# Second product of expert 0: seven products of token pairs for three of four batches, with the sums on GpSimd

## The chip, the cores and the metric

The kernel runs on 1 core of one Trainium2 chip. The metric is device time in microseconds (us); less is better. The engines are called as in the profile: PE (TensorE matmuls), PEld (TensorE weight loads), DVE (VectorE), ACT (ScalarE), POOL (GpSimd) and SP (SyncE).

## The reference

Block-sorted attention for 4 batches of 768 tokens, 8 heads of 64, is followed by a mixture of 8 experts in which every token goes through every expert, weighted by a balanced gate.

```python
def _attn_ref(q, k, v, sort_net):
    P = sort_net
    for _ in range(5):                       # softmax over rows, then columns summed to one
        ...
    k_sorted = np.einsum('bhij,bhjcd->bhicd', P, k_b).reshape(B, H, S, D)
    v_sorted = np.einsum('bhij,bhjcd->bhicd', P, v_b).reshape(B, H, S, D)
    ...                                      # softmax attention inside each block of 96 tokens

def _moe_ref(x, w_gate, w1, w2):             # x is [3072, 512]
    P = np.exp(x @ w_gate - max)
    for _ in range(8):                       # rows to one, columns to one, times N / E
        ...
    for e in range(E):
        h = np.maximum(x @ w1[e], 0.0)       # [3072, 1024]
        out += P[:, e:e + 1] * (h @ w2[e])   # [3072, 512]
```

## The kernel before

Matmuls take bf16 operands; results are gathered in float32 in SBUF, 24 tiles `osbl[:, t, :]` of 128 tokens and 512 columns, six to a batch.

**Stages.** Attention of the four batches comes first. Each batch is a list of steps in `attention`: `queries` (q0 to q3), `keys`, `scores`, `mix`, `turn` and `logits`, one of each for a pair of heads. In batches 2 and 3 (counted from 0) `queries` first has GpSimd copy a pair of heads into a small tile `qr` (two buffers), which TensorE then transposes. `sort_values` makes the sorted values of the next batch and sends them through eight DMAs (`vsb`, four issued by GpSimd, four by SyncE). `load_batch` and `load_w1`/`load_w2` are DMAs issued by GpSimd.

Expert 0 is woven into attention: `first_two` yields its steps for batches 0 and 1, in halves of 384 tokens, and `weave` takes a given number of them (`ns`) between attention steps. `hidden0` makes one block of 128 hidden features for 384 tokens (4 matmuls of 384 columns, then relu on ScalarE); `output0` makes one tile of results with 8 matmuls of 512 columns, in two steps of four. `keep` copies a result tile from PSUM to `osbl`. Batches 2 and 3 of expert 0 come after attention, in `last_two`, beside the gate's balancing (`balance`, a chain of small VectorE operations and matmuls), and batch 3's output is interleaved step by step with part of the first hidden stage of expert 1.

Experts 1 to 7 already multiply 2x2 blocks with seven products in place of eight (Strassen-Winograd) in both their products. The block sums that this needs are made on GpSimd for w1 (`sum_w`), w2 (`sum_w2`) and h (`sum_h`, tiles `hs`), and on VectorE for x (`sum_x`). `output7` makes two result tiles, `a` and `b`, out of seven products of 4 matmuls of 256 columns each.

**What sets the order.** Each engine runs its own instructions in the order of its queue. `pin` keeps an instruction in the order in which the program writes it; GpSimd's DMAs, copies for `build_r`, w1 and w2 sums are pinned, and so are most matmuls. `tc.issue_after` holds the first weight loads behind one copy. Before the w2 sums of expert 1 a pinned copy `held <- glog` (line 644) makes GpSimd wait for the balance, and `sums(8)` stands behind it at step 40 of the loop over `last_two`.

**The steady loop.** After that, for each of 21 passes (an expert and a third of the tokens), the outputs of one pass run beside the hidden steps of the next. In expert 1's passes `scale0` multiplies expert 0's result tiles by the gate, on ScalarE, for the tiles not yet multiplied when they were kept.

Of the kernel before, what the change touches and what calls it, by code (L numbers as in the profile page):

```python
# [1 line left out]

_os.environ.setdefault("NEURON_RT_ULTRASERVER_MODE", "4")
# [10 lines left out]
F32 = mybir.dt.float32  # L14
BF16 = mybir.dt.bfloat16
AF = mybir.ActivationFunctionType
AX = mybir.AxisListType
ALU = mybir.AluOpType
# [7 lines left out]
def kernel(  # L26
# [11 lines left out]
    nc = tc.nc  # L38
# [9 lines left out]
    wp = ctx.enter_context(tc.tile_pool(name="wp", bufs=2))  # L48
    wcp = ctx.enter_context(tc.tile_pool(name="wcp", bufs=1))
    xtp = ctx.enter_context(tc.tile_pool(name="xtp", bufs=1))  # L50
    actx = ExitStack()
    mps = actx.enter_context(tc.tile_pool(name="mps", bufs=2))
    kvp = actx.enter_context(tc.tile_pool(name="kvp", bufs=2))
# [30 lines left out]
    def load_w2(e):  # L84
        w2t[e] = (wq if e else wcp).tile([128, 8, Dm], BF16, name="w2e")
        pin(nc.gpsimd.dma_start(out=w2t[e],
                                in_=moe_w2[e].rearrange("(fb k) f -> k fb f", k=128)))
# [32 lines left out]
        nc.vector.reciprocal(out=cs, in_=cs)  # L120
        nc.vector.tensor_mul(Pt, Pt, mkap(cs, [cs.ap[0], cs.ap[1], [0, 8]]))

    Prep = perp.tile([32, 8, 8, 16], BF16)
    for eng, i0 in ((nc.vector.tensor_copy, 0), (nc.scalar.copy, 4)):
        eng(Prep[:, i0:i0 + 4], mkap(P, [P.ap[0], [8, 4], [1, 8], [0, 16]], off=i0 * 8))

    xtT = xtp.tile([128, 4, N], BF16)
    osbl = xtp.tile([128, NT, Dm], F32)
    glog = xtp.tile([128, NT, E], F32)
    xc = {0: xtp.tile([128, 3, 2, 512], BF16, name="xc0")}  # L130

# [166 lines left out]
            yield  # L298


    def hidden0(c0, hTs, hbank):
        for fb in range(8):
            hps = hbank()
            for kk in range(4):
                pin(nc.tensor.matmul(hps[:, 0:384], w1t[0][:, kk, fb * 128:(fb + 1) * 128],
                                     xtT[:, kk, c0:c0 + 384], start=(kk == 0), stop=(kk == 3)))
            nc.scalar.activation(out=hTs[:, fb, 0:384], in_=hps[:, 0:384], func=AF.Relu)  # L307
            yield

    def output0(c0, hTs, obank, done):  # L310
        for tt in range(3):
            oacc = obank()
            for fb in range(8):
                pin(nc.tensor.matmul(oacc, hTs[:, fb, tt * 128:(tt + 1) * 128],
                                     w2t[0][:, fb, :], start=(fb == 0), stop=(fb == 7)))
                if fb == 3:
                    yield
            done(c0 // 128 + tt, oacc)
            yield

    def keep(t, oacc):
        (nc.vector.tensor_copy if t < 12 else nc.scalar.copy)(osbl[:, t, :], oacc)

    def keep_scaled(t, oacc):
        nc.scalar.activation(out=osbl[:, t, :], in_=oacc, func=AF.Copy,
                             scale=glog[:, t, 0:1])

    wct = {}

# [36 lines left out]
    def weave(a, b, na, nb):  # L366

        t = 0
        for i in range(na):
            next(a, 0)  # L370
            while t * na < (i + 1) * nb:
                next(b, 0)
                t += 1

    with ExitStack() as c2:
        pa = c2.enter_context(tc.tile_pool(name="pa", bufs=8, space=bass.MemoryType.PSUM,
                                           reuse_waits="tile"))
        bank1 = lambda shape, dt: pa.tile(shape, dt, name="bank", tag="bank")
        ebank = lambda: bank1([128, 512], F32)
        def first_two():  # L380
            for c0 in range(0, 2 * S, 384):
                hTs = mps.tile([128, 8, 384], BF16, name="hTs")
                yield from hidden0(c0, hTs, ebank)
                yield from output0(c0, hTs, ebank, keep)

        ex = first_two()
        for _ in range(12):
            next(ex)
        for bb, ns in ((1, (5, 3, 3, 5)), (2, (5, 3, 2, 4)), (3, (5, 4, 0, 5))):
            at1 = attention(bb, bank1)  # L390
            weave(at1, ex, 5, ns[0])
            if bb + 1 < B:
                load_batch(bb + 1, [(x, 0, 8) for x in "vkq"])
                build_r(bb + 1, nc.gpsimd, 4)
            else:
                load_w1(1)
                sums = sum_w(1)
            weave(at1, ex, 3, ns[1])
            if bb + 1 < B:
                weave(sort_values(bb + 1, bank1), ex, 5, ns[2])  # L400
            else:
                for _ in sums:
                    pass
                x0 = sum_x(0)
                for _ in range(3):
                    next(x0)
            weave(at1, ex, 4, ns[3])
        for _ in ex:
            pass
# [2 lines left out]

    late = lambda name, bufs: ctx.enter_context(
        tc.tile_pool(name=name, bufs=bufs, reuse_waits="tile"))
    mpc, xcp, wq, wcq = late("mpc", 1), late("xcp", 2), late("wq", 2), late("wcq", 1)
    htp, fsp, hsp, w2q = late("htp", 2), late("fsp", 1), late("hsp", 3), late("w2q", 1)
    h3p = late("h3p", 2)
    bk = ctx.enter_context(tc.tile_pool(name="bk", bufs=5, space=bass.MemoryType.PSUM,
                                        reuse_waits="tile"))
    op = ctx.enter_context(tc.tile_pool(name="op", bufs=3, space=bass.MemoryType.PSUM,  # L420
                                        reuse_waits="tile"))
    load_w2(1)

    def bank():
        return bk.tile([128, 512], F32, name="bk")

    w2s = {}

    def sum_w2(e):
        w2s[e] = (w2q.tile([128, 4, 4, Dm // 2], BF16, name="w2s") if e % 2 else  # L430
# [104 lines left out]
        yield  # L535

    def gather(e, t, c, ps):
        o = osbl[:, t, c:c + ps.shape[-1]]
        nc.vector.scalar_tensor_tensor(out=o, in0=ps, scalar=glog[:, t, e:e + 1], in1=o,  # L539
                                       op0=ALU.mult, op1=ALU.add)  # L540

    def store(e, t):
        if e == E - 1:
            nc.sync.dma_start(out=out[t * 128:(t + 1) * 128, :], in_=osbl[:, t, :])

    hs = {}

    def sum_h(i, hT, f0=0, f1=4):

        if f0 == 0:  # L550
            hs[i] = hsp.tile([128, 3, 4, 128], BF16, name="hs")
        s1, s2, s4 = (hs[i][:, j, f0:f1] for j in range(3))
        a11, a21, a12, a22 = (hT[:, f + f0:f + f1, t + 128 * i:t + 128 * i + 128]
                              for f in (4, 0) for t in (0, 512))
        for a, b, o, c in ((a21, a22, ALU.add, s1), (s1, a11, ALU.subtract, s2),
                           (a12, s2, ALU.subtract, s4)):
            nc.gpsimd.tensor_tensor(out=c, in0=a, in1=b, op=o)  # L557
# [40 lines left out]

    def scale0(ts):
        for t in ts:  # L600
            nc.scalar.activation(out=osbl[:, t, :], in_=osbl[:, t, :], func=AF.Copy,
                                 scale=glog[:, t, 0:1])

    def units(e, p, hT, hold=lambda ins: ins):
        for i in range(4):
            yield from hidden(e, p, i, hT, hold)
# [7 lines left out]
            else:  # L614
                queue.pop(0)

    def last_two():
        for bb, done in ((2, keep), (3, keep_scaled)):
            hT = htp.tile([128, 8, 1024], BF16, name="hT")
            halves = [(bb * S + c, hT[:, :, c:c + 384]) for c in (0, 384)]  # L620
            for c0, hTs in halves:
                yield from hidden0(c0, hTs, bank)
            for c0, hTs in halves:
                yield from output0(c0, hTs, lambda: op.tile([128, Dm], F32, name="oacc"), done)

    tail0, chain = last_two(), balance()
    x1, x2 = sum_x(1), sum_x(2)
    works = {0: x0, 10: x1, 14: x1, 19: x1, 23: x1, 41: x2, 43: x2, 46: x2, 48: x2}
    first = None
    for n in range(56):  # L630
        next(tail0)
        if n == 28:
            hT = htp.tile([128, 8, 1024], BF16, name="hT")
            first = units(1, 0, hT, pin)
        if first:
            next(first)
            if n == 28 + 21:
                sum_h(0, hT, 0, 3)
        if n in works:
            next(works[n], 0)  # L640
        if n in (0, 2, 4, 6, 8, 11, 13, 15, 17, 20, 22, 24, 26, 29, 31, 33, 35, 37, 39):
            next(chain)
        if n == 40:
            pin(nc.gpsimd.tensor_copy(held, glog[0:96, NT - 1, 0:2]))
            sums(8)

    hTs = {0: hT}

# [8 lines left out]
    for n in range(1, 3 * (E - 1) + 1):  # L657
        e, p, hT = 1 + (n - 1) // 3, (n - 1) % 3, hTs[n - 1]
        d = 2 + n // 3
        fetch = n == 1 or n % 3 == 0 and d < E  # L660
        if fetch:
            load_w1(d)
            queue.append(sum_w(d))
        for i in range(4):
            if e == 1:
                scale0([t for t in (8 * p + i, 8 * p + 4 + i) if t < 18])
            if i == 0:
                sum_h(0, hT, 3)
            if i < 3:
                sum_h(i + 1, hT)  # L670
            elif n < 3 * (E - 1):
                sum_h(0, hTs[n], 0, 3)
            sums(1 + i // 2)
            for _ in output7(e, p, i, hT):
                next(ahead, 0)
        if fetch:
            load_w2(d)
            queue.append(sum_w2(d))
# [30 lines left out]
```

## Time and profile before

| what | value |
|---|---|
| median of 3 runs | 681.02 us (680.26 to 682.88) |
| the profiled execution | 680.63 us, of which 678.7 us from first to last instruction |
| PE busy | 654.8 us (96%) |
| DVE, ACT, POOL busy | 544.7, 298.5, 472.4 us |
| mean granted TensorE clock | 0.991 |
| attention of batch 1, 2, 3 starts | 45, 70, 93 us |
| attention ends, late part of expert 0 begins | 114 us |
| steady loop begins | 171 us |
| one pass of the steady loop | 24.3 us |

The times of the stages are read from the order of the matmuls in the timeline: transposes of queries open a batch's attention, and the last hidden matmul of the 28 that run beside batch 3's output closes the late part. All times inside the profile count from the start of the span.

### The profile page before, as it was taken

What the parts mean: (1) busy time and instruction counts of PE and PEld (TensorE: products, weight loads), DVE (VectorE), ACT (ScalarE), POOL (GpSimd) and SP (SyncE); (2) the same over time, 40 slices, a digit from 0 to 9 for tenths busy, and PEclk for the clock granted to TensorE, in tenths of its full rate; (3) what the DMA queues carried; (4) which work ended last, traced back from release to release, by engine and by line L of the source; (5) the groups of instructions that cost most, each with busy time, mean ns of one, the idle gap of its engine ahead of it and who ended that gap; (6) DMA issues with size and microseconds to landing.
All of it is one profiled execution on the core that took longest, in us unless ns stands there. A gap on an engine that the chain in (4) does not pass through costs nothing.

```text
span 678.7 us, 13239 instructions
## 1 busy us (share of the span) xinstructions
PE 654.8 (96%) x5108; PEld 436.7 (64%) x5108; DVE 544.7 (80%) x1154; ACT 298.5 (44%) x550; POOL 472.4 (70%) x499
## 2 busy tenths in 40 slices
PE   2989999999999999999999999999999999999996
PEld 1756766554666666666666666666666666666665
DVE  6727768663788889888888888888898888988885
ACT  3757764469533343434334343333433334333330
POOL 4542335007987988898997898689887989645744
PEclk9799999999999999999999999999999999999999
DMA  9898972101240340030303040034003220001223
GB/s 145 165 218 130 153 125 44 26 1 19 44 63 1 63 63 2 1 63 11 54 1 58 6 63 1 3 61 63 1 2 63 28 36 0 1 1 64 94 94 125
DMA packets 31759, 36.57 MB, mean 54 GB/s; under 512 B 2000, under 2 KB 24016, under 8 KB 31696
## 3 DMA queue, kind: packets, MB, share of 16 engines
q0 software_dynamic: 26400, 27.82, 25.8%
q1 hardware_dynamic: 5296, 7.90, 3.4%
q8 instruction: 40, 0.66, 0.4%
q14 instruction: 23, 0.19, 0.1%
HBM read 52.45 MB, written 6.29 MB: 87 GB/s over the span
## 4 chain that ended last, share of the span: by engine, by line
PE 72%; DVE 1%; POOL 1%; issue 0%; ACT 0%
PE oacc L572 37%; PE bk L487 35%; DVE osbl L539 1%; POOL hs L557 1%; DVE hT L523 0%; DVE hT L526 0%; ACT p L507 0%
## 5 line engine op out<-in xcount | busy, mean ns | idle before, releaser
L539 DVE SCALAR_TENSOR_TENSOR osbl<-oacc,glog,osbl 128x256 f32<-128x256 f32 (+1 forms) x504 | 262.4, 523 | 62.5 <-PE oacc L572 62.2
L487 PE MATMUL bk<-xtT,w1e 128*128 128x512 bf16 x504 | 149.7, 379 | 0.0
L557 POOL TENSOR_TENSOR hs<-hT 128x512 bf16<-128x512 bf16 (+2 forms) x105 | 99.6, 961 | 67.9 <-DVE hT L526 67.8
L572 PEld LDWEIGHTS <-hT 128*128 128x128 bf16 x1008 | 98.6, 98 | 64.8 <-issue 1.3
L572 PEld LDWEIGHTS <-hs 128*128 128x128 bf16 x1008 | 98.4, 98 | 64.2 <-POOL hs L557 1.5
L572 PE MATMUL oacc<-w2e,hT 128*128 128x256 bf16 x816 | 123.1, 273 | 0.8 <-ACT hT L529 0.5
L529 ACT ACTIVATE hT<-bk 128x512 bf16<-128x512 f32 x84 | 50.3, 599 | 158.2 <-PE bk L487 158.2
L557 POOL TENSOR_TENSOR hs<-hT,hs 128x512 bf16<-128x512 bf16 (+2 forms) x105 | 100.0, 959 | 4.9
L557 POOL TENSOR_TENSOR hs<-hs,hT 128x512 bf16<-128x512 bf16 (+2 forms) x105 | 100.0, 960 | 4.3 <-ACT hT L529 0.4
L487 PE MATMUL bk<-xc,wc 128*128 128x512 bf16 x336 | 99.9, 379 | 0.2 <-ACT p L507 0.2
L572 PE MATMUL oacc<-w2e,hs 128*128 128x256 bf16 x624 | 93.8, 273 | 0.9 <-POOL hs L557 0.9
L515 ACT COPY u<-bk 128x512 f32<-128x512 f32 x84 | 49.3, 587 | 95.4 <-PE bk L487 93.2
L487 PEld LDWEIGHTS <-w1e 128*128 128x128 bf16 x672 | 65.8, 98 | 10.4
L523 DVE CUSTOM_DVE_ANT_0 hT<-bk,p 128x512 bf16<-128x512 f32 x84 | 58.1, 692 | 11.5 <-ACT p L520 6.4
L533 DVE SCALAR_TENSOR_TENSOR h<-bk,hT 128x512 bf16<-128x512 f32 x84 | 57.2, 681 | 5.7 <-ACT hT L529 5.7
L520 ACT COPY p<-bk 128x512 f32<-128x512 f32 x84 | 49.4, 588 | 23.2 <-PE bk L487 23.2
L507 ACT COPY p<-bk 128x512 f32<-128x512 f32 x84 | 49.4, 588 | 20.3 <-PE bk L487 20.3
L511 DVE CUSTOM_DVE_ANT_0 hT<-bk,p 128x512 bf16<-128x512 f32 x84 | 57.2, 681 | 0.9 <-ACT hT L307 0.5
L526 DVE CUSTOM_DVE_ANT_0 hT<-bk,u 128x512 bf16<-128x512 f32 x84 | 57.1, 680 | 1.0 <-PE bk L487 1.0
L572 PE MATMUL oacc<-w2s,hs 128*128 128x256 bf16 x384 | 57.5, 273 | 0.1
L487 PEld LDWEIGHTS <-wc 128*128 128x128 bf16 x504 | 49.3, 98 | 8.0 <-issue 0.4
L487 PE MATMUL bk<-xc,w1e 128*128 128x512 bf16 x168 | 50.0, 379 | 0.0
(110 smaller groups left out, 820.6 us busy)
## 6 DMA issues: line engine op xcount, KB each, us to landing
w1e<-in_moe_w_dram POOLq DMA_DIRECT2D x8, 1024.0 KB, 8.2
w2e<-in_moe_w_dram POOLq DMA_DIRECT2D x8, 1024.0 KB, 9.0
out_dram<-osbl SPq DMA_DIRECT2D x24, 256.0 KB, 2.0
kvq<-in_v_dram POOLq DMA_DIRECT2D x3, 768.0 KB, 10.3
vsb<-vs SPq DMA_DIRECT2D x16, 97.5 KB, 4.7
vsb<-vs POOLq DMA_DIRECT2D x16, 97.5 KB, 4.3
kvq<-in_q_dram POOLq DMA_DIRECT2D x4, 384.0 KB, 13.0
kvq<-in_k_dram POOLq DMA_DIRECT2D x4, 384.0 KB, 13.6
```

The lines of the kernel that those rows point to most:

```text
L487: hold(nc.tensor.matmul(ps, wa[:, kk, :], xa[:, kk, :], start=(first and kk == 0), stop=(kk == 1), skip_group_check=True))
L507: nc.scalar.copy(p1, u)
L511: nc.vector._custom_dve(TENSOR_ADD_SAT, out=c11, in0=w, in1=p1, s0=TOP, s1=0.0)
L515: nc.scalar.copy(u2, u)
L520: nc.scalar.copy(p5, v)
L523: nc.vector._custom_dve(TENSOR_ADD_SAT, out=c22, in0=u, in1=p5, s0=TOP, s1=0.0)
L526: nc.vector._custom_dve(TENSOR_ADD_SAT, out=c12, in0=v, in1=u2, s0=TOP, s1=0.0)
L529: nc.scalar.activation(out=c21, in_=u, func=AF.Relu)
L533: nc.vector.scalar_tensor_tensor(out=h3[e, p][:, i, :], in0=u, scalar=0.0, in1=c22, op0=ALU.max, op1=ALU.subtract)
L539: nc.vector.scalar_tensor_tensor(out=o, in0=ps, scalar=glog[:, t, e:e + 1], in1=o, op0=ALU.mult, op1=ALU.add)
L557: nc.gpsimd.tensor_tensor(out=c, in0=a, in1=b, op=o)
L572: nc.tensor.matmul(ps, h[:, fb, :], w[:, fb, :], start=(first and fb == 0), stop=(fb == 3), skip_group_check=True)
```

## The change

For batches 1, 2 and 3, the second product of expert 0 (h times w2) takes seven products per pair of result tiles in place of `output0`. A pair is a tile of the batch's first 384 tokens and the one at the same place in its second 384. Batch 0 keeps `output0`.

- `sum_w2_0` makes the sums of w2 of expert 0 on GpSimd: six as soon as the values of batch 2 are sorted, two more, written over a part of w2 itself, when the next step of `first_two` is asked for.
- `sum_h0` makes four sums for each pair on GpSimd. For the pair 0 of batch 1 they come in two halves, after the fourth and the eighth hidden block of the second half batch (`each`).
- `pair0` and `pairs0` make the products, `put` copies a result to `osbl`, `more` adds to it. If the gate is balanced by then (`gated`), both also multiply by it.
- Hidden blocks go in the order 0, 4, 1, 5, 2, 6, 3, 7; the numbers of steps woven into attention of batches 2 and 3 are larger.
- The late part first makes the hidden stages of batches 2 and 3, then the pairs of batch 2, then batch 3's pairs interleaved with 28 hidden steps of expert 1. `sums(8)` (w2 of expert 1) is written ahead of it all, and the copy `held <- glog` is gone. The balance and x sums are placed by a running count of nominal microseconds (`went`).
- The last six result tiles are a tile of their own, in memory that attention has left (`osbl[1]`).

```diff
+    def sum_w2_0():
+        w2s[0] = wcq.tile([128, 3, 4, Dm // 2], BF16, name="wc")
+        last = []
+        for k in (0, 2):
...
+            for a, b, c in ((b12, b11, t1), (b22, t1, t2), (b21, t2, t4)):
+                pin(nc.gpsimd.tensor_tensor(out=c, in0=a, in1=b, op=ALU.subtract))
+            last.append((b22, b12))
+        yield
+        for b22, b12 in last:
+            pin(nc.gpsimd.tensor_tensor(out=b12, in0=b22, in1=b12, op=ALU.subtract))
+
+    def sum_h0(bb, i, hA, hB, f0=0, f1=4):
+        if f0 == 0:
+            hs0[bb, i] = pool_hs()
...
+        for a, b, o, c in ((a21, a22, ALU.add, s1), (s1, a11, ALU.subtract, s2),
+                           (a11, a21, ALU.subtract, a21), (a12, s2, ALU.subtract, s4)):
+            pin(nc.gpsimd.tensor_tensor(out=c, in0=a, in1=b, op=o))
...
+    def pair0(bb, i, hA, hB, obank, eng):
...
+        add(u, hA[:, 4:8, cs], b11, True)
+        put(a, 0, u, eng)
+        yield
+        add(x0, hA[:, 0:4, cs], b21, True)
+        yield
+        add(x1, s1, t1, True)
+        put(b, 256, x1, nc.scalar)
+        yield
+        add(u, s2, t2, False)
+        put(a, 256, u, nc.scalar)
+        yield
+        add(x1, s4, b22, False)
+        more(a, 0, x)
+        yield
+        add(u, s3, t3, False)
+        more(b, 256, u)
+        yield
+        add(u, hB[:, 0:4, cs], t4, False)
+        put(b, 0, u, nc.scalar)
+        yield
+
+    def pairs0(bb, hA, hB, obank, eng, behind):
+        p = [pair0(bb, i, hA, hB, obank, eng) for i in range(3)]
+        for n, i in enumerate((0, 0, 0, 0, 0, 1, 0, 1, 0, 1, 1, 1, 2, 1, 2, 1, 2, 2, 2, 2, 2)):
+            next(p[i])
+            if n == 8:
+                behind(0)
+            elif n == 15:
+                behind(1)
+            yield
+        behind(2)
...
         def first_two():
-            for c0 in range(0, 2 * S, 384):
-                hTs = mps.tile([128, 8, 384], BF16, name="hTs")
+            half = lambda: mps.tile([128, 8, 384], BF16, name="hTs")
+            for c0 in (0, 384):
+                hTs = half()
                 yield from hidden0(c0, hTs, ebank)
                 yield from output0(c0, hTs, ebank, keep)
-
+            next(s20, 0)
+            hA, hB = half(), half()
+
+            def each(n):
+                if n in (3, 7):
+                    sum_h0(1, 0, hA, hB, (n - 3) // 2, (n + 1) // 2)
+
+            yield from hidden0(S, hA, ebank)
+            yield from hidden0(S + 384, hB, ebank, each)
+            sum_h0(1, 1, hA, hB)
+            yield from pairs0(1, hA, hB, ebank, nc.vector,
+                              lambda i: sum_h0(1, 2, hA, hB) if i == 0 else None)
+
+        s20 = sum_w2_0()
...
-        for bb, ns in ((1, (5, 3, 3, 5)), (2, (5, 3, 2, 4)), (3, (5, 4, 0, 5))):
+        for bb, ns in ((1, (5, 3, 3, 5)), (2, (6, 4, 3, 5)), (3, (7, 4, 0, 8))):
...
                 weave(sort_values(bb + 1, bank1), ex, 5, ns[2])
+                if bb == 1:
+                    next(s20)
...
+    sums(8)
+    for bb in (2, 3):
+        for _ in hid(bb):
+            went(0.65)
+        if bb == 2:
+            for i in range(3):
+                sum_h0(2, i, *hh[2])
+    for _ in pairs0(2, *hh[2], obank, nc.scalar, lambda i: sum_h0(3, i, *hh[3])):
+        went(0.436)
+    hT = htp.tile([128, 8, 1024], BF16, name="hT")
+    first = units(1, 0, hT, pin)
+    n = 0
+    left = pairs0(3, *hh[3], obank, nc.scalar, lambda i: None)
+    for m in range(28):
+        next(first)
+        went(0.436)
+        if m == 20:
+            sum_h(0, hT, 0, 3)
+        while n * 28 < (m + 1) * 21:
...
+            next(left)
+            n += 1
+            went(0.436)
```

## The prediction

> **What bounds the kernel now.** I read the page first: busy times, the slices, and the DMA table.
>
> ```profile
> PE 654.8 (96%) x5108; PEld 436.7 (64%) x5108; DVE 544.7 (80%) x1154; ACT 298.5 (44%) x550; POOL 472.4 (70%) x499
> ...
> PE   2989999999999999999999999999999999999996
> ...
> POOL 4542335007987988898997898689887989645744
> ...
> w1e<-in_moe_w_dram POOLq DMA_DIRECT2D x8, 1024.0 KB, 8.2
> w2e<-in_moe_w_dram POOLq DMA_DIRECT2D x8, 1024.0 KB, 9.0
> ```
>
> TensorE (PE) is busy in every slice but the first and last; the chain of waits that ended last runs on PE matmuls almost alone from 173 to 655 us. So PE work removed is time gained, and a PE wait added is time lost. GpSimd (POOL) has its free slices (0, 0) at 119 to 153 us, just where much of the new work goes. So I read the timelines of both engines from 65 to 171 us, POOL first.
>
> ```profile
> 65.00 2.14 POOL L170 DMA_DIRECT2D vsb<-vs  x4 [1.57 <-ACT vs L163]
> 70.58 1.60 POOL L188 COPY qr<-kvq 128x768 bf16<-128x768 bf16 x2 [3.45 <-PE bank L192]
> ...
> 73.92 0.90 POOL L72 DMA_DIRECT2D kvq<-in_q_dram  x1
> ...
> 88.24 1.59 POOL L188 COPY qr<-kvq 128x768 bf16<-128x768 bf16 x2 [11.33 <-PE bank L241]
> ...
> 94.82 0.81 POOL L81 DMA_DIRECT2D w1e<-in_moe_w_dram  x1
> 103.80 1.15 POOL L338 TENSOR_TENSOR wc<-w1e 128x512 bf16<-128x512 bf16 x1 [8.17 <-DMA w1e<-in_moe_w_dram]
> ...
> 112.91 0.94 POOL L86 DMA_DIRECT2D w2e<-in_moe_w_dram  x1
> 152.91 0.18 POOL L644 CAST held<-glog 96x2 bf16<-96x2 f32 x1 [39.07 <-DVE glog L475]
> ```
>
> Columns: start, length, instruction, idle time before it. POOL takes its work strictly in this order: attention's small `qr` copies, the batch loads, then expert 1's weights and their sums. Its 39.07 us of rest come after all of that.
>
> ```profile
> 72.87 0.51 PE L192 MATMUL bank<-Ibig,qr 128*128 128x128 bf16 x6
> ...
> 95.57 0.51 PE L192 MATMUL bank<-Ibig,qr 128*128 128x128 bf16 x6
> ...
> 128.98 4.48 PE L314 MATMUL oacc<-w2e,hT 128*128 128x512 bf16 x20
> ...
> 170.71 0.59 PE L487 MATMUL bk<-xc,w1e 128*128 128x512 bf16 x2
> ```
>
> PE transposes the third `qr` of batch 2 at 72.87 and of batch 3 at 95.57; the POOL copy for the first of these ended by 72.12, so POOL is only some 0.7 us early. The last line is the last of expert 1's first 28 hidden steps; it ends at 171.14, where the steady loop begins.
>
> **What it removes.** From the timeline 20 matmuls of 512 columns take 128.98 to 133.30, 0.216 us each; four of 256 columns take 0.434 us (173.91 to 174.35). A batch now takes 48 of the first, 10.4 us; then 3 pairs x 7 products x 4 of the second, 9.1 us. Three batches save 3 x 1.28 = 3.8 us of PE.
>
> **What it adds on POOL.** Eight sums of w2 and 40 of h. Their prices:
>
> ```profile
> L557 POOL TENSOR_TENSOR hs<-hT 128x512 bf16<-128x512 bf16 x63 | 72.2, 1153 | 0.0
> ...
> L557 POOL TENSOR_TENSOR hs<-hT 128x384 bf16<-128x384 bf16 x21 | 19.2, 915 | 43.2 <-DVE hT L526 43.2
> ...
> L557 POOL TENSOR_TENSOR hs<-hT 128x128 bf16<-128x128 bf16 x21 | 9.0, 430 | 24.7 <-DVE hT L526 24.5
> ```
>
> In a row, 8 of 512 take 9.11 us (103.80 to 112.91), 1.14 each. The form with 256 elements isn't shown; its neighbours bound it by 0.43 and 0.92, and I take the line between, 0.67 (0.65 in a row). What matters is where these stand in POOL's queue, which I followed instruction by instruction in the changed program.
>
> **Step 1, attention of batch 2.** The eight w2 sums stand behind the four `vsb` DMAs and ahead of the copies of the third and fourth `qr`. DMAs end at 67.14, the sums at 67.14 + 9.11 = 76.25 (the last two also wait for PE's old-form output, which ends at 69.95, in time). The third `qr` is ready at 77.05. PE, with one hidden step (0.65) more ahead of it, gets there at 73.5: it waits 3.6 us. Behind the same queue the loads of batch 3 slip: the q load from 73.92 to 79.6.
>
> **Step 2, attention of batch 3.** The q load took 13.8 us to land, so now 93.4. POOL then does, in order: two `qr` copies (95.0); the first half of pair sums (1,0) (four of 0.65, 97.6); the `vsb` DMAs (99.8); the other half (102.4; its first sum 100.5); pair sums (1,1) (4.58, 107.0); only then the third `qr`, 107.8. Its inputs from PE are earlier: the last hidden step of the batch is through at about 96. PE without waits: value sorting moves from 84.16 to 84.16 + 3.6 + two more hidden steps 1.3 = 89.1; before, it was 8.5 from there to the first `qr` (92.65); with 6 hidden steps (3.9) and 2 products (0.9) for 6 half tiles (5.2) that is 8.1, so 97.2. From the first `qr` to the third it was 2.9; one hidden step leaves and two products come, 3.1, so 100.3. PE can pass there only at 107.9: it loses 7.6 us, of which 2.1 at the product that needs the first sum. Attention ends at 114.04 - 1.3 + 3.6 + 7.6 = 123.9.
>
> **Step 3, POOL becomes the path.** Pair sums (1,2) need a buffer that PE frees at 108.8; they end at 113.4. Only behind them is the load of w1 of expert 1 issued. It takes 9.0 (94.82 to 103.80), 122.4; eight sums 9.1, 131.5; the w2 load 9.0, 140.5; eight sums 9.6 (as at 153.06 to 162.65), 150.1; twelve sums for batch 2, 13.8, 163.9. PE is through its 32 hidden groups at 123.9 + 12.6 (as 114.04 to 126.60) + 10.7 (16 x 0.65 and two balance matmuls) = 147.2, and 0.9 later needs the first of these sums, ready at 151.3. From there three pairs want 3.0 us each from PE and 4.6 each from POOL. The last sum frees a 0.43 us product; the batch's last product follows two DVE adds (0.75 and 0.48, by the result adds of 128x512 and 128x256) with a 0.5 reduce of the balance between: batch 2 is done at 166.5, where PE alone would have been done at 156.6.
>
> **Step 4, the mixed stretch.** 28 hidden steps and 21 products of 0.434 and two small balance matmuls (0.14): 21.6 us, to 188.1. The sums of batch 3 end at 163.9 + 13.8 = 177.7, each ahead of its product (the third pair's at about 182). DVE has some 18 us of work in it, hidden by a little; without that cover an extra 1 to 2 us. ACT copies of 128x256 (between nothing and the 0.59 of 128x512) have room: ACT is under half busy.
>
> **The rest at nothing.** The fourth sum of `x0` ran at 85.1 already (0.68 on DVE), so writing it earlier in the text moves nothing. Without the `held` copy nothing ties expert 1's w2 sums to the balance: they start earlier than 152.91, which is in step 3. The other order of the hidden steps has the same price. In the steady loop (24.3 us a pass) four more `scale0` tiles lie on ACT (0.77 each, 9.4 us busy of 24.3), and the last result tiles' other place costs no instruction. Moving the start from 171.14 to 188.1 adds 16.9. Profiled execution: 680.63 + 16.9 = 697.5. The median lies 0.39 above that execution, so 697.9. Ends of the sum: if w1 lands in 8.2 and the half sums cost 0.43, 3 us less; DVE late in the mixed stretch, 2 more.
>
> **Rivals.** First, all sums hidden: 681.0 - 3.8 = 677.2, faster. The 39.07 us of rest speak for it. It decides at PE's third `qr` of batch 2: eight sums would have to end by 72.7, under 0.7 us each, where the row says 1.14. And 48 new ones come to some 50 us, more than the rest. Second, POOL is late in attention only and catches up in its rest: 681.0 - 3.8 + 3.6 + 7.6 = 688.4. Against it: two loads in series with their sums stand ahead of batch 2's sums, 50 us from 113.4. It would need the w1 load ahead of the pair sums. Third, the clock:
>
> ```profile
> 22.00:24.00 2.00, 1.04 (x31) 0.79 (x26) 0.50 (x2) 2.00 (x6) 0.51 (x1) 1.00 0.63 169
> ...
> 26.00:28.00 2.00, 2.00 (x22) 1.74 (x22) 2.00 (x9) 1.00 (x3) 2.00 (x4) 0.50 0.52 47
> ```
>
> These are 2 us windows (PE busy second, granted clock third from the end): after gaps the clock fell to 0.50 from 25 to 35 us, up to 5 us lost. The new gaps (3.6, 5.5, 3.2 us) could do the same. While POOL is the path, slow matmuls hide in PE's 9.9 us of waiting; they cost only if they reach past 166.5: then 697.9 + 5 = 702.9. [...] Fourth, losses and gain happen to cancel: 681.
>
> **Chances.** Forecast 0.70, clock 0.13, late in attention only 0.08, all hidden 0.06, cancel 0.03. Range 688 to 703: from the second rival to the third. A difference of 0.5% (3.4 us) is about what a measurement can tell; 677.2 lies just past it, so faster 0.05, within 0.04, slower 0.91.
>
> **What would show it.** Right: PE idle some 3 to 4 us near 74 until a POOL `qr` copy, 5 us near 102 to 108 until another; the w1 load of expert 1 issued near 113 rather than 95; sums of batch 2 at 150 to 164 back to back, with PE waiting on POOL between; the steady loop from 188. Wrong: PE dense from 65 to 165, or the w1 load issued before 100; or a granted clock of 0.5 after 166. If PE waits at 74 and 105 but not at 150, step 3 is wrong alone.

## The result, and the profile after

The changed kernel takes 709.62 us (706.24 to 710.63 in four runs); the kernel before, run beside it, takes 681.90 us (680.26 to 682.88). The ratio is 1.0405 (95% interval 1.0385 to 1.0425). The direction was forecast, the size was not: 697.9 with a range up to 703 were predicted, and 11.7 us are missing. The profiled execution took 709.61 us, of which 707.8 from first to last instruction.

The first fence answers the page's busy times and slices of before.

```profile
PE 658.8 (93%) x5147; PEld 450.7 (64%) x5216; DVE 564.8 (80%) x1169; ACT 305.9 (43%) x575; POOL 524.5 (74%) x546
...
PE   3999786896899999999999999999999999999996
...
POOL 3533856589288898889888899969996999646644
```

PE has lost its row of nines between the fifth and the eleventh slice (some 71 to 195 us). Of POOL's long rest at 119 to 153 us two waits for loads are left, 7.2 us before 125.7 and 8.0 before 143.7; it now rests for 12.4 us before 194.6.

POOL's timeline, in the columns of before, is what the prediction followed by hand:

```profile
69.06 1.18 POOL L344 TENSOR_TENSOR wc<-w2e 128x512 bf16<-128x512 bf16 x1
...
79.21 1.59 POOL L195 COPY qr<-kvq 128x768 bf16<-128x768 bf16 x2
...
82.55 0.90 POOL L75 DMA_DIRECT2D kvq<-in_q_dram  x1
...
110.43 1.59 POOL L195 COPY qr<-kvq 128x768 bf16<-128x768 bf16 x2
...
117.62 0.81 POOL L84 DMA_DIRECT2D w1e<-in_moe_w_dram  x1
...
153.47 1.15 POOL L359 TENSOR_TENSOR hs<-hT 128x512 bf16<-128x512 bf16 x1
```

Forecast were 67.1, 76.3, 79.6, 107.0, 113.4 and 150.1: POOL runs as predicted, 2 to 4 us late. The next fence has the lines of PE's timeline that end a wait of over 1 us from 70 to 190 us; the bracket gives the wait and its releaser.

```profile
80.09 0.82 PE L199 MATMUL bank<-Ibig,qr 128*128 128x128 bf16 x6 [4.34 <-POOL qr L195]
103.98 1.14 PE L388 MATMUL bank<-wc,hs 128*128 128x256 bf16 x6 [1.55 <-POOL hs L359]
111.31 0.82 PE L199 MATMUL bank<-Ibig,qr 128*128 128x128 bf16 x6 [5.24 <-POOL qr L195]
129.24 0.60 PE L388 MATMUL bank<-wc,hTs 128*128 128x256 bf16 x4 [1.62 <-DVE osbl L376]
161.79 0.39 PE L585 MATMUL bk<-cs,onesc 128*128 128x8 f32 x2 [1.79 <-DVE cs L582]
167.18 0.60 PE L388 MATMUL oacc<-w2e,hT 128*128 128x256 bf16 x4 [1.07 <-DVE osbl L376]
173.18 0.60 PE L388 MATMUL oacc<-wc,hT 128*128 128x256 bf16 x4 [2.89 <-DVE osbl L376]
180.70 0.59 PE L601 MATMUL bk<-xc,w1e 128*128 128x512 bf16 x2 [2.01 <-DVE hT L637]
```

The three waits on POOL were forecast (3.6, 2.1 and 5.5 us). The five waits on DVE were not, and the forecast waits of the pairs on POOL after 150 us don't exist. Why DVE is late is in its groups by line (count, busy time, mean ns of one), first the balance of before (114 to 153 us), then of after (133 to 190 us):

```profile
L468 DVE TENSOR_REDUCE cs<-glog 128x8 f32<-128x192 f32 x8 | 4.0, 499 | 0.3
...
L467 DVE TENSOR_TENSOR glog<-glog,rs 128x192 f32<-128x192 f32 x8 | 2.8, 356 | 0.2
...
L465 DVE TENSOR_SCALAR rs<-rs 128x24 f32<-128x24 f32 x8 | 1.4, 174 | 0.2
```

```profile
L581 DVE TENSOR_TENSOR glog<-glog,rs 128x192 f32<-128x192 f32 x8 | 7.4, 931 | 0.3
...
L579 DVE TENSOR_SCALAR rs<-rs 128x24 f32<-128x24 f32 x8 | 4.6, 576 | 0.2
L582 DVE TENSOR_REDUCE cs<-glog 128x8 f32<-128x192 f32 x8 | 4.0, 495 | 0.2
```

The same instructions on the same sizes take 931 in place of 356 ns and 576 in place of 174, while the reduce takes 495 as before. The other product (`glog` times `cs`) goes from 358 to 763. With the rows that stay (reduces 353 and 499, reciprocals 303 and 203, 164), an iteration's VectorE work grows from 2.4 to 3.8 us. In the stretch of batch 2's pairs this is what fills the time; the second line is the mixed stretch behind it (batch 3's pairs between hidden steps of expert 1):

```profile
157.03:173.83 16.80, 10.84 (x90) 8.56 (x89) 15.04 (x29) 4.60 (x14) 16.57 (x14) 1.00 0.00 0
...
173.83:200.87 27.04, 24.03 (x145) 14.75 (x147) 17.83 (x32) 20.12 (x42) 11.99 (x13) 0.94 0.06 9
```

(Columns: stretch, length, then busy time and count of PE, PEld, DVE, ACT and POOL; the granted clock is the third number from the end.) In the pairs PE is busy 10.8 of 16.8 us, DVE 15.0 and POOL 16.6. Nobody waits for POOL there; PE waits for DVE.

### The profile page after: what moved, and what is told of

Same layout as the page of the kernel before. It is cut to its first block, busy times and chain, and to the rows that moved or that the text cites. A ratio compares the mean times of both kernels' runs of the same rounds, so it can differ in the third digit from the quotient of the medians.

```text
span 707.8 us, 13488 instructions
## 1 busy us (share of the span) xinstructions
PE 658.8 (93%) x5147; PEld 450.7 (64%) x5216; DVE 564.8 (80%) x1169; ACT 305.9 (43%) x575; POOL 524.5 (74%) x546
## 4 chain that ended last, share of the span: by engine, by line
PE 69%; ACT 1%; DVE 1%; issue 1%; POOL 1%; ACTq 0%
PE oacc L686 36%; PE bk L601 33%; DVE osbl L653 1%; ACT osbl L715 1%; POOL hs L671 1%; ACT osbl L366 0%; ACT u L629 0%; PE oacc L388 0%; DVE hT L637 0%; DVE hT L640 0%; ACT p L621 0%; ACT p L634 0%; ACT osbl L368 0%; ACT hT L643 0%; ACTq L629 0%
## 5 line engine op out<-in xcount | busy, mean ns | idle before, releaser
L653 DVE SCALAR_TENSOR_TENSOR osbl<-oacc,glog,osbl 128x256 f32<-128x256 f32 (+1 forms) x504 | 262.2, 523 | 61.8 <-PE oacc L686 61.4
L601 PE MATMUL bk<-xtT,w1e 128*128 128x512 bf16 x477 | 144.8, 381 | 1.3 <-ACT u L629 0.2
L601 PE MATMUL bk<-xc,wc 128*128 128x512 bf16 x317 | 95.9, 380 | 0.8 <-ACT p L621 0.4
L601 PEld LDWEIGHTS <-w1e 128*128 128x128 bf16 x672 | 65.9, 98 | 12.6 <-issue 3.6
L601 PE MATMUL bk<-xc,w1e 128*128 128x512 bf16 x159 | 48.2, 379 | 2.4 <-DVE hT L637 2.3
## 6 DMA issues: line engine op xcount, KB each, us to landing
kvq<-in_v_dram POOLq DMA_DIRECT2D x3, 768.0 KB, 11.2
kvq<-in_q_dram POOLq DMA_DIRECT2D x4, 384.0 KB, 12.8
```

The costliest lines, as they stand in the source:

```text
L601: hold(nc.tensor.matmul(ps, wa[:, kk, :], xa[:, kk, :], start=(first and kk == 0), stop=(kk == 1), skip_group_check=True))
```

## The experiments

Each number is a median with its ratio to the kernel before on the same chip. "Steady loop" is the end of the 28th hidden step of expert 1 (171.1 us before, 200.9 in the changed kernel), and "mixed" the stretch up to it.

| run | us | ratio (95%) | attention, us | hidden stages | pairs of batch 2 | mixed | steady loop |
|---|---|---|---|---|---|---|---|
| before | 681.0 | 1 | 44.1 | | | | 171.1 |
| changed | 709.6 | 1.0405 (1.0385 to 1.0425) | 61.8 | 23.4 | 16.8 | 27.0 | 200.9 |
| e1_before_idle_sums | 691.7 | 1.0153 (1.0132 to 1.0174) | | | | | 181.8 |
| e2_no_late_sums | 700.2 | 1.0275 (1.0259 to 1.0292) | 61.1 | 25.1 | 11.9 | 23.4 | 192.5 |
| e3_balance_in_psum | 701.8 | 1.0300 (1.0282 to 1.0318) | 62.2 | 22.7 | 14.6 | 23.4 | 192.9 |
| e4_queue_order | 696.4 | 1.0224 (1.0185 to 1.0264) | 47.6 | 24.6 | 18.0 | 26.5 | 186.7 |
| e5_fill_the_gaps | 707.5 | 1.0399 (1.0371 to 1.0428) | 61.5 | 24.0 | 18.1 | 26.3 | 202.3 |
| e6_order_and_psum | 690.0 | 1.0133 (1.0117 to 1.0149) | 47.6 | 25.9 | 14.2 | 23.4 | 180.8 |
| e7_all_removed | 689.0 | 1.0113 (1.0090 to 1.0137) | 46.3 | 22.0 | 12.6 | 27.9 | 180.7 |
| e8_last_product_apart | 708.7 | 1.0398 (1.0377 to 1.0419) | 58.7 | 28.1 | 17.8 | 26.1 | 201.2 |
| e9_balance_early | 692.7 | 1.0167 (1.0153 to 1.0181) | 47.0 | 22.7 | 13.5 | 25.3 | 178.9 |
| e10_balance_in_sbuf | 697.9 | 1.0240 (1.0226 to 1.0254) | 47.0 | 24.4 | 14.6 | 28.3 | 184.9 |
| e11_late_batches_only | 680.7 | 0.9993 (0.9984 to 1.0002) | 44.1 | 22.5 | 11.4 | 23.7 | 174.0 |
| e12_three_batches_best | 685.4 | 1.0062 (1.0048 to 1.0076) | 47.6 | 22.7 | 11.4 | 23.7 | 176.6 |

Stages are read from the timeline of PE in the profiled execution: attention from the first query transpose of batch 2 to the first hidden step behind attention, the hidden stages of batches 2 and 3 up to the first product, the pairs up to the first hidden step of expert 1. The first query transpose of batch 2, ahead of all that is changed, comes at 69.7 to 72.3 us (71.9 or later in the four profiles with 17 us of an early half clock), so the last column is uncertain by some 2 us. In the changed kernel, e2 to e6, e11 and e12 three matmuls of the following steps (0.65 us) stand ahead of the end of the 28th step, and some matmul records are missing (the changed kernel's page has 5147 matmuls for 5216 weight loads), so the end of a stage is good to about 0.7 us.

**Is it GpSimd's sums that slow VectorE?** The kernel before gets 27 subtractions on GpSimd in its rest, whose result nobody uses:

```diff
     load_w2(1)
+    scr = hsp.tile([128, 3, 4, 128], BF16, name="hs")
+    pin(nc.gpsimd.memset(scr[:, 0], 0.0))
+    for _ in range(27):
+        pin(nc.gpsimd.tensor_tensor(out=scr[:, 1], in0=scr[:, 0], in1=scr[:, 0],
+                                    op=ALU.subtract))
```

> The kernel before, with 27 extra GpSimd sums of 128x512 bf16 on a scratch tile, unused by anything, in the time in which GpSimd rests (113 to about 145 us) and the balance runs on VectorE. Nothing else is changed. Theory A (GpSimd's sums hold up VectorE instructions that read two operands from SBUF, or go from SBUF to SBUF as tensor-scalar): the balance's product of the gate with the row factors rises from 0.36 to about 0.9 us, the small tensor-scalar from 0.17 to about 0.6, TensorE waits for the balance, and the kernel gets slower by 2 to 4 us. Theory B (the longer balance of the changed kernel comes from how its work is queued): those means stay at 0.36 and 0.17, the time within 1 us.

It costs 10.5 us, more than the 2 to 4 that were expected. Groups of DVE from 113 to 150 us in this run:

```profile
L139 DVE TENSOR_TENSOR xc<-xtT,xc 128x1024 bf16<-128x1024 bf16 x4 | 5.7, 1472 | 0.0
...
L472 DVE TENSOR_TENSOR glog<-glog,rs 128x192 f32<-128x192 f32 x6 | 4.8, 802 | 0.2
```

The x sums take 1472 ns where they took 678 in the same stretch before (both inputs in SBUF), and the balance slows as in the changed kernel. PE's wait lines show what it costs:

```profile
122.67 0.55 PE L459 MATMUL bk<-gm,onesc 1*128 1x1 f32 x2 [4.14 <-DVE gm L456]
...
138.57 0.36 PE L476 MATMUL bk<-cs,onesc 128*128 128x8 f32 x2 [2.52 <-DVE cs L473]
```

No product, load or queue of the change is in this kernel: sums on GpSimd alone hold PE up by way of VectorE. The expectation had the mechanism, but not that four slow x sums (116.6 to 122.3 us) stand ahead of the balance's second maximum. Some 2.1 of the 10.5 us are an indirect price: the clock fell to 0.50 with the first wait (0.83 is the mean from 115 to 135 us), and the next 16 matmuls of 384 columns took 4.9 us where they took 2.8 before.

**How much are the late sums of h?** The changed kernel without the 24 sums of batches 2 and 3; their products read other tiles, so the output differs there.

```diff
 def sum_h0(bb, i, hA, hB, f0=0, f1=4):
+    if bb > 1:
+        return
```

> The changed kernel without the 24 sums of h of batches 2 and 3: their products read blocks of h as they are, so this part of the computation is left out. In the changed kernel the stretch from the last hidden matmul before batch 2's pairs to expert 1's first hidden step takes 16.8 us where its matmuls need 9.4. Theory A: the stretch falls to 10 to 11 us, the VectorE operations in it go back to 0.36 and 0.17 us, and the total falls by 7 to 12 us from the changed kernel's 709.6. Theory B (VectorE has too much queued ahead of the result adds, sums or not): the stretch stays above 14, the total falls by under 4 us.

It takes 9.5 us less. The pairs fall from 16.8 to 11.9 us and the mixed stretch from 27.0 to 23.4; attention moves by 0.7 us. The balance's product with the row factors takes 0.36 us again in six of its eight iterations, and 0.93 and 0.92 in the two that run beside the w2 sums of expert 1. That doesn't tell yet whether POOL's place on the path (step 3) or its effect on DVE is the cause.

**POOL on the path, or DVE slowed?** All sums stay; the row and column factors of the balance move to PSUM, so that each of its products has one operand left in SBUF.

```diff
-        rs2 = mpc.tile([128, NT], F32)
-        cs1 = mpc.tile([128, E], F32)
         for it in range(8):
+            rs2 = bank()[:, 0:NT]
...
             csps = bank()[:, 0:128]
+            cs1 = csps[:, 64:64 + E]
```

> The changed kernel with one difference: the row factors and column factors of the balance are kept in PSUM and not in SBUF, so that the balance's products read one operand from SBUF and one from PSUM. All sums stay. Theory A: the two products of the balance fall from 0.93 and 0.76 to about 0.4 us, the stretch of batch 2's pairs from 16.8 to 10 to 12 us, the total by 5 to 9 us. Theory B: no change beyond 1 us.

7.9 us less. A group of DVE and two wait lines of PE:

```profile
L580 DVE TENSOR_TENSOR glog<-glog,bk 128x192 f32<-128x192 f32 x8 | 2.8, 352 | 0.2
```

```profile
157.54 0.61 PE L388 MATMUL oacc<-w2e,hs 128*128 128x256 bf16 x4 [0.71 <-POOL hs L359]
...
166.67 0.61 PE L388 MATMUL oacc<-w2e,hs 128*128 128x256 bf16 x4 [1.06 <-POOL hs L359]
```

The product is back at 352 ns with every sum of POOL running beside it. Now PE waits for POOL's sums in the pairs, 2.7 us in three waits: step 3's path exists, right behind DVE's, and is worth little because PE arrives late.

**The queue in attention.** The changed kernel with GpSimd's order changed: the w2 sums behind the loads of batch 3, three `qr` copies of batch 3 as soon as their data lands (three buffers), the first pair's sums in one piece, the w1 load ahead of the last sums of batch 1.

```diff
-            next(s20, 0)
...
+                if bb == 2:
+                    for _ in s20:
+                        pass
+                    for hp in range(3):
+                        copy_q(3, hp)
...
+            for n in range(21):
+                if n == 5:
+                    sum_h0(1, 1, hA, hB)
+                elif n == 10:
+                    sum_h0(1, 2, hA, hB)
+                next(left1)
+                yield
```

> The changed kernel with another order in GpSimd's queue during attention and nothing else: the sums of w2 stand behind the batch loads, the copies of three of batch 3's query pairs ahead of the sums of h, the fourth ahead of the second pair's sums, the load of w1 of expert 1 ahead of the third pair's. Theory A (the waits for these copies, and the half clock that follows each, cost what the changed kernel loses in attention): no wait over 1 us for a query copy, no clock of 0.5 between 70 and 120 us, attention ends near 114 to 117 and not at 133.7; the late part still waits for sums and for VectorE; total down by 10 to 16 us from 709.6. Rival: the late part's chain of sums on GpSimd sets the time anyway, so that only 3 to 7 us come back.

13.2 us less (its four runs spread from 693.7 to 700.3). Both waits on `qr` are gone and attention takes 47.6 us, not 61.8; the late stages stay slow. This run has the contention inside one timeline: POOL rests from 123 to 131.41 us and then begins its w2 sums. Lines of DVE (start, length):

```profile
129.90 0.36 DVE L595 TENSOR_TENSOR glog<-glog,rs 128x192 f32<-128x192 f32 x1
...
134.42 0.92 DVE L595 TENSOR_TENSOR glog<-glog,rs 128x192 f32<-128x192 f32 x1
```

**The clock behind the waits.** Matmuls that nobody reads fill the two waits for `qr`.

```diff
+            if hp == 2:
+                dps = bank([128, 512], F32)
+                for _ in range(16 if bb == 2 else 20):
+                    pin(nc.tensor.matmul(dps, w1t[0][:, 0, 0:128], w1t[0][:, 1, 0:512],
+                                         start=True, stop=True))
```

> The changed kernel with matmuls whose results nobody reads put ahead of the third query transposes: 16 in batch 2, 20 in batch 3 (512 columns, 0.216 us each, so 3.5 and 4.3 us inside waits of 4.3 and 5.2 us). Everything else stays. Theory (the clock falls behind each long wait, and the slow stretch counts): the granted clock stays at 1.00 from 78 to 118 us, where it was 0.50 to 0.87 at 78 to 84 and 110 to 118; attention ends 3 to 5 us earlier than at 133.7, the whole is 705 to 707 us against 709.6. Rival (the slow matmuls stand beside GpSimd's queue, which sets the time of what follows): attention ends earlier but the whole stays at 709 to 710.

2.1 us less, with intervals that overlap: neither shown nor excluded. Both expectations had attention end earlier, and it ends at 133.8 (the profiled execution is the slowest of the four, 711.0). Two windows of the changed kernel, then two of this run (granted clock is the third number from the end):

```profile
80.00:82.00 2.00, 1.91 (x10) 1.07 (x10) 0.00 (x0) 0.80 (x1) 2.00 (x4) 0.50 0.00 0
112.00:114.00 2.00, 2.00 (x26) 1.30 (x25) 0.93 (x2) 0.80 (x1) 0.96 (x2) 0.50 0.03 8
```

```profile
80.00:82.00 2.00, 1.51 (x22) 1.01 (x22) 0.02 (x1) 0.97 (x2) 2.00 (x3) 1.00 0.00 0
...
104.00:106.00 2.00, 1.69 (x12) 0.97 (x14) 0.00 (x0) 0.56 (x2) 1.92 (x4) 0.50 0.53 128
```

The first fall is avoided, but the clock now falls in the wait for the first sum of h (2.75 us here, up to 104.3; 0.94 from 102 to 104 us, 0.50 from there to 110). The filling matmuls of batch 3 run at half speed until 110.6, so that their row ends at 113.2, over a us past the `qr` copy that PE was waiting for (ready by about 111.6). Attention takes 61.5 us against 61.8. Half clock inside attention adds up to 6.8 us here, 10.2 in the changed kernel and 13.7 in e2, with attention at 61.5, 61.8 and 61.1: its length doesn't follow the slow clock there, as if slow matmuls stood mostly beside POOL's queue.

**Both causes together.** e4 and e3 in one kernel.

> The two edits tried singly before together: GpSimd's queue reordered in attention (13.2 us gained alone) and the two small operands of the balance in PSUM (7.9 us gained alone). Theory (two separate causes, one in attention, one on VectorE behind it): the gains add up, 688 to 690 us. Rival (with attention on time, GpSimd's sums of h become what the pairs of batch 2 wait for, as step 3 of the prediction had it, and the gain of the second edit is lost again): 692 to 696, with PE waits on GpSimd of 4 us or more between 140 and 165.

690.0 us, 19.6 less than the changed kernel, where the two alone give 21.1: two causes that nearly add up, at the edge of the theory's 688 to 690. PE waits for POOL's sums in the pairs as in e3, 2.3 us and not the rival's 4.

**What is left.** e6, with batch 2's and 3's sums of h ahead of expert 1's w2 sums, the first pair's in halves, the x sums and the balance pinned on VectorE, a later chain, and the last product of a pair in the PSUM of the second one. There it starts a fresh sum, so the left half of tile `b` lacks the terms of the earlier products; the instructions are the same.

```diff
-        add(u, hB[:, 0:4, cs], t4, False)
-        put(b, 0, u, nc.scalar)
+        add(x0, hB[:, 0:4, cs], t4, True)
+        put(b, 0, x0, nc.scalar)
...
-    sums(8)
...
+    times = [(0.0, chain), (3.0, chain), (5.0, chain)]
+    times += [(6.81 + 4.1 * n, xs) for n in (0, 1, 2, 3, 4, 5, 6, 7)]
```

> Both edits, and: GpSimd makes the sums of h of batches 2 and 3 ahead of the sums of w2 of expert 1, the first pair's in two halves; the last product of a pair goes to the half of PSUM that the second one used, so that it no longer waits for the add of the sixth; the x sums and the balance keep the order of the program on VectorE, one x sum behind each first half of an iteration, and the chain starts 1.6 to 2.6 us later. Theory (the loss was waits only, all of them named): less than 4 us of PE waits remain between 65 and 190 us and the time comes to 677 to 682, level with the kernel before or below. Rival (GpSimd's sums still slow VectorE's x sums, which then hold up the balance and the result adds): 684 to 690.

689.0, the rival's range. The hidden stages and pairs are the better for it (22.0 and 12.6 us), but the mixed stretch takes 27.9: PE waits 3.1 us for one add, through which VectorE works without a pause, on the balance, a hidden result and last a pinned x sum of 0.89 us, and the clock falls behind that wait (0.94 is the mean from 160 to 190 us, where e6 has 1.00).

**The last product's place alone.** The first four lines of that diff, on the changed kernel, with the same terms left out.

> The changed kernel with one edit: the last product of a pair (t4) goes into the half of PSUM that the second product used, which is free one product and one add earlier. Theory (PE's waits on the result adds, 1.6, 0.7, 1.1 and 2.9 us at the ends of batches 1 and 2, count in full): half to all of these 6.3 us are gone, 703 to 706.5 us against 709.6. Rival (VectorE is late as a whole there, so PE waits for it at the next place): 708.5 to 710.

0.9 us less, within the runs' spread: the rival's number. The waits did count where they stood, as attention takes 58.7 us and not 61.8. But the balance then begins earlier, while POOL still makes the sums of w1: four x sums take 6.1 us (129.6 to 135.6) where they took 3.2 in the changed kernel, PE waits 3.0 us for the second maximum behind them, and the hidden stages grow from 23.4 to 28.1 us. The gain is lost again to the same contention.

**The balance over before the mixed stretch, and back in SBUF.** e9 makes the sixth product ahead of the fifth and spaces iterations by 3.4 us; e10 is e9 with the two operands back in SBUF.

```diff
-        times += [(6.8 + 4.1 * n, chain), (9.3 + 4.1 * n, chain)]
+        times += [(6.0 + 3.4 * n, chain), (8.5 + 3.4 * n, chain)]
...
+    times += [(12.81, xs)] + [(t, xs) for t in (60, 61, 62, 63)]
```

> All edits of e7 except the last product's place; instead the sixth product (s3, t3) is made ahead of the fifth (s4, b22), so that the last one waits only for a 0.41 us add and has a product of 0.43 us in between. Three x sums stand in the pauses at the start of the balance, one behind its third iteration, the four of the last third behind everything, and the iterations follow each other in 3.4 us in place of 4.1, so that the balance is over when the mixed stretch has begun. VectorE then has some 17 us of work in the mixed stretch, where e7 left it 24 us against 22 us of matmuls. Theory (in e7 VectorE was the bound of the mixed stretch): the waits of 3.1 and 0.6 us and the half clock behind them go, 680 to 684 us. Rival (iterations of 3.4 us are too short for the chain and PE waits for each column sum): 686 to 690.

> e9 with the two small operands of the balance back in SBUF, nothing else. Theory (GpSimd's sums slow VectorE's instructions whose operands all lie in SBUF, wherever they stand in the program): the three instructions of an iteration take 0.58, 0.93 and 0.76 us in place of 0.18, 0.35 and 0.35, an iteration of 2.5 us becomes 3.9, and PE waits for the column sums: 5 to 8 us above e9. Rival (the slow instructions are VectorE's own, or the reordering has already taken their weight): within 1.5 us of e9.

e9 misses both its numbers: 692.7. Its mixed stretch is shorter (25.3), but the four x sums that were put off stand in a row at the start of the steady loop, 1.4 to 1.6 us each, and PE waits 1.3 and 1.8 us for the adds behind them; the exchanged products bring new waits on ScalarE. The comparison it was made for is clear: e10 is 5.3 us above it, and among the totals of PE's waits from 60 to 210 us stands in e10

```profile
PE bk L601 <- DVE cs L598: 4.4, 4, 2.3
```

where e9 has

```profile
PE bk L601 <- DVE cs L597: 0.3, 1, 0.3
```

(total, times, longest). Two small operands (24 and 8 columns) make these 5 us, in an order that was made to suit the balance. The three instructions took 346, 609 and 594 ns in e10 from 118 to 165 us, less than expected, as POOL rests for a part of that time.

**Which batches pay?** e11 makes batch 1 in the old form, and the w2 sums behind the w2 load; a second PSUM pool serves the first tile of each pair of batch 2, and the x sums are spread over the mixed stretch. e12 is the same late part with all three batches.

```diff
+    both = itertools.cycle((bank, obank))
-    for _ in pairs0(2, *hh[2], obank, ...
+    for _ in pairs0(2, *hh[2], lambda: next(both)(), ...
...
+    times += [(12.81, xs)] + [(t, xs) for t in (36, 40, 44, 48)]
```

> Seven products only in batches 2 and 3, behind attention; batch 1 in the old form, so that attention is that of the kernel before, with the w1 load at 95 us. GpSimd: the w2 sums of expert 0 behind the w2 load (113 to 123 us), the sums of h of batches 2 and 3 from about 124 to 153, then the w2 sums of expert 1. Balance in PSUM, in the order of e9 (3.4 us an iteration), the fifth and sixth product in the original order, a second PSUM pool for the first tile of each pair of batch 2, x sums of the last third spread over the mixed stretch. Theory (attention's loss came from batch 1's sums and its small steps; what is lost behind attention are waits on VectorE that all of this removes): attention ends at 114 as before, the steady loop starts at 169 to 171.5, and the time is 678.5 to 682, within 0.4% of the kernel before. Rival (VectorE stays late in the pairs whatever the order, as GpSimd's sums slow it there): 684 to 688.

> e9 with the fifth and sixth product back in the original order, the second PSUM pool for the first tile of each pair of batch 2, and the x sums of the last third spread over the mixed stretch: the late part of e11 with the attention of e4. Theory (each stage has its own price): 3 to 5 us above e11, the price of attention (23.4 us from the first queries of batch 3 to its end in e9 where it was 21.4 before), 683 to 686, and 6 to 9 below e9. Rival (the waits move on): 688 or more.

Both times came out as the theory had it: 680.7, level with the kernel before, and 685.4. (The steady loop of e11 begins later than its 169 to 171.5, as its batch 2 begins at 72.3 where the kernel before has 69.95.) Of e11's waits from 60 to 210 us one group is above half a microsecond:

```profile
PE bk L390 <- DVE osbl L378: 0.7, 1, 0.7
```

Attention takes 44.1 us in e11 as before, and 47.6 in e12, where it should have been 1.3 shorter: batch 1's form costs 4.8 us in attention even without a wait for `qr`, 2.3 of them in waits on result adds. From the end of attention to the end of the span e11 needs 564.3 us and the kernel before 564.7; two batches should have saved 2.6. The rest goes in small gaps: from 147 to 170 us PE is busy 21.7 of 23 us, where it was 23.0 before. VectorE is busy 17.8 us there (10.6 before) and ScalarE 19.6 (21.2), so it is VectorE that got the added work; that its adds make the gaps is likely but not shown.

## Why the prediction was wrong, step by step

Two terms of the sum failed. Step 2 let batch 1's seven products save 1.3 us inside attention, and they cost 3.5 there. Steps 3 and 4 took VectorE's instructions at the length that they have while GpSimd rests; that GpSimd's sums slow them stood in the sum at nothing, and it measured 7.9 us on the balance alone (e3), without which the kernel comes to 701.8, inside the range.

**Savings.** Right as rows: four matmuls of 256 columns take 0.43 us in the changed kernel too. e11 and e12 show that next to nothing of it arrives.

**Step 1.** Right: eight w2 sums in 10.2 us for 9.1, a wait of 4.34 for 3.6.

**Step 2.** Right for the waits (5.24 and 1.55 for 5.5 and 2.1), wrong for the end of attention, 133.7 for 123.9. This is the largest miss, and the first in time. Of the 9.8 us, 1.9 lie ahead of the change (an early half clock, 17.1 us in all there and 10.2 in the kernel before) and 0.7 in the first wait, while the waits of batch 3 came out 0.8 shorter. Another 4.8 are the term "- 1.3": with no wait for `qr` and no fall of the clock in attention, e12, with GpSimd's queue in e4's order, takes 47.6 us there against 44.1 with batch 1 in the old form (e11), so the term is + 3.5. The waits on result adds (1.62 and 0.68) are part of it. The runs don't take the last 3.2 us apart; slow clock behind the waits can be in them, but e2, e5 and the changed kernel don't show attention longer with more of it. e4 prices the queue order at 13.2 us; the prediction's price for it was 11.2 (3.6 and 7.6).

**Step 3.** Wrong. POOL kept its times (3.4 us late at the first of batch 2's sums), but PE reached the pairs at 157.0, not 147.2, and by then the sums were ahead of it. The prediction's own sign came true: waits that begin near 76 and 106 us, none on POOL at 150. The stretch took 16.8 us, and that this is near the 19.3 forecast is luck: what filled it was DVE's slowed balance. e3 shows POOL's path come up once DVE is relieved.

**Step 4.** Wrong, 27.0 us for 21.6. "DVE has some 18 us of work in it, hidden by a little; without that cover an extra 1 to 2 us" was right in the amount, 17.8 us, but took single instructions' lengths from a trace in which POOL rested. The balance's products take 1.04 and 1.25 us at 176 to 180 us, PE waits 2.0 us for VectorE behind them, and 3.4 us of half clock follow, a loss of 1.7; the rest are waits of under 0.4 us and the three matmuls ahead of the mark. Price of the contention in whole kernels: 7.9 us alone (e3), 6.4 beside the reordered queue (e4 to e6), 5.3 in e9 to e10, and 10.5 by itself with its half clock (e1).

The sum closes: the steady loop began at 200.9 for 188.1, 12.8 us late, out of 9.8 in attention, 0.1 in the hidden stages, 2.5 less in the pairs and 5.4 in the mixed stretch.

**The clock rival.** Right in kind: the clock fell to 0.50 in both long waits (at 79.5 and 110.2 us) and again at 181.9. It was restored after 3.4, 6.8 and 3.4 us. e5 moved a fall as well as avoiding one, so it doesn't settle what the falls in attention cost; the 1.7 us at 182 to 185 count.

**VectorE beside GpSimd's sums.** The traces tell it row by row: the balance's product took 931 ns against 356 with both inputs in SBUF, and 352 with one of them in PSUM (e3); the reduce took 495 against 499; POOL's sums lengthened as well (1.60 us at times, for 1.15). The prediction counted POOL's sums in POOL's and PE's time only.

## What to carry to other kernels

Work for an idle engine isn't free because the engine is idle: ask which rows of the profile were measured while it rested, and price every neighbour's instruction again for the time when it works (356 ns became 931 here). When a chain of small operations sets the pace, the memory in which its small operands lie can be worth more than its order (7.9 us in e3, 5.3 between e9 and e10). Before moving sums to GpSimd, follow its queue: a load or a copy that stands behind them moves all later stages (13.2 us in e4).

## What the runs showed of the hardware that was not expected

- Beside GpSimd's sums VectorE's `tensor_tensor` with both inputs in SBUF took 1472 in place of 678 ns (128x1024, e1) and 931 in place of 356 (128x192, the changed kernel), its `tensor_scalar` from SBUF to SBUF 576 in place of 174; with the row factors in PSUM (e3) the last two took 352 and 190.
- The granted clock fell to 0.50 in or shortly behind waits of 2.01 (the changed kernel) and 2.75 us (e5) as well as in those of 4.34 and 5.24 (the changed kernel), and came back after 3.4 or 6.8 us.
- The length of a wait alone doesn't decide: in the changed kernel the wait of 2.89 us up to 173.2 left the clock at 1.00, and behind that of 2.01 us up to 180.7 it fell. The four falls of this execution from 20 to 200 us, at 24.87, 79.48, 110.20 and 181.88, lie 54.61, 30.72 and 71.68 us apart, which are 16, 9 and 21 times 3.41.
- An early half clock came to 3.4 us in all in e4 and e8, to 10.2 in the kernel before (from 24.5 us) and to 17.1 in the changed one (from 24.9); in e8 the clock is 1.00 from 24 to 34 us and 0.83 from 34 to 44. The four profiles with 17 us (changed, e5, e7, e11) begin batch 2 at 71.9 to 72.3 us; the kernel before, e2 to e4, e6, e8 to e10 and e12 begin it at 69.7 to 71.2.
